# A codec kernel with a fixed task order, four groups of x per transposing transfer, a fourth residual buffer and the third tap's products on Pool

## The chip, the cores and the metric

The kernel runs on one core of one Trainium2 chip. The metric is device time in microseconds (us), from the first to the last work of one execution. Before the change three runs gave 812.22, 815.28 and 817.3 us, so the median is 815.28 us. Engines are named as in the profile: PE (TensorE matmul), PEld (its weight loads), DVE (VectorE), ACT (ScalarE), POOL (GpSimd) and SP (SyncE, which here only issues transfers).

## The reference

```python
B, T, D, K = 2, 16000, 512, 3
Nq, C = 4, 8
xp = jnp.pad(x, ((0,0),(pad,pad),(0,0)))
for i in range(K):
    z = z + xp[:, i:i+T, :] * dw_enc[i][None, None, :]
res = z = silu(z)
for s in range(Nq):
    cb = codebooks[s]
    d2 = einsum("btd,btd->bt", res, res)[..., None] - 2.0 * einsum("btd,cd->btc", res, cb) + einsum("cd,cd->c", cb, cb)
    idx = d2.argmin(-1)
    sel = cb[idx]
    q = q + sel
    res = res - sel
# qp = q padded like x
for i in range(K):
    y = y + qp[:, i:i+T, :] * dw_dec[i][None, None, :]
```

All tensors are bf16. A three-tap convolution per channel and a SiLU make z; four residual quantisers each pick the nearest of 8 code words; a second three-tap convolution per channel runs over the sum of the picked words.

## The kernel before

**Tiling.** The 32,000 tokens are cut into 250 groups of 128 tokens, token p of group g being row 250 p + g of x, so that neighbours in time lie in neighbouring groups. The groups form 17 chunks: `SIZES` gives 4, 12, fourteen times 16, and 10. Channels lie on the partitions, in four blocks of 128, so one operation on one block of a 16-group chunk has the shape 128x2048.

**Loading.** Chunks 0 and 1 come in as rows and are turned on PE. From chunk 2 on, each group is a transposing transfer of its own on SP's queue (L428), into the ring `XT` of 34 groups. When the ring wraps, POOL copies two groups to its start (L444).

**Front of a chunk**, for each of the four channel blocks: three products of x with a tap (L486: tile Z for the first, T for the second and third, all on DVE); two additions into Z or into the residual (L500 on DVE, or an accumulating transfer Z<-T that POOL issues, L497); exp on ACT (L508), plus one on DVE (L512), reciprocal on ACT (L184), and the product with that (L518 on DVE), which leaves the SiLU in a residual buffer `RES`. `SPLIT = (1, 1, 1, 2)` says how many of the two additions are transfers in each block: five of eight in a chunk, so three are L500.

**Four stages of a chunk**, one after the other, since each needs the residual of the one before. PE computes the products of each token with itself and with the code words (the scores, L590, after a mask matmul, L584), in two halves of 8 groups. ACT takes the diagonal out (L601), DVE casts the dot products (L620), PE adds up (L604, L611), DVE casts the sums (L616). POOL adds the code norms (L658), makes a small tie-break term (L645 adds a norm, L647 multiplies), and adds both (L662). DVE takes the minimum (L666) and the one-hot (L672), POOL notes it (L678). PE and ACT turn the one-hots into picks of word pairs (L715, L720, L727, L733); PE multiplies these by the code words (L749) and DVE adds the result to the residual (L755, four per stage, in stages 0 to 2). After stage 3 the one-hots are turned (L701) and PE decodes the output with two or three matmuls per group pair (L773), ACT copies it out (L779) and SP stores it (L783).

**Buffers.** `RES` is a set of three buffers. A chunk takes one at its first L500 and gives it back when its stage-3 scores are done. Z, T and E have four tiles each, PSUM four.

**Order.** `Plan` holds the tasks of all chunks with an estimated hold and delay. It steps through time and gives each free engine the ready task with the earliest due time, `START[chunk] + OFF[name]`, if its buffers are free. What comes out is a fixed order on each engine. Where PE would idle, the planner adds warm-up matmuls (L387), with `WARM = 0.4`.

Of the kernel before, what the change touches and what calls it, by code (L numbers as in the profile page):

```python
# [10 lines left out]
BF16 = mybir.dt.bfloat16  # L11
# [9 lines left out]
LC = 16  # L21
ROOM = 2 * GC + 2

SIZES = [4, 12] + [16] * 14 + [10]
# [5 lines left out]
WARM = 0.4  # L30
SPLIT = (1, 1, 1, 2)
RELU = (0, 1, 2, 3)

ZB, TB, EB, YB = 4, 4, 4, 2
# [3 lines left out]
START = [-49.78, -21.21, -11.1, 40.29, 77.41, 126.87, 171, 213.64, 259.89, 295.9, 339.35, 382.88, 414.63, 449.59, 490.48, 512.46, 542.77]  # L38
OFF = {
    "words": -209.08, "codes": -112.52, "col0": -187, "sums": -87.73, "mask": -228.88, "norms": -202.91, "col1": 18.74,  # L40
# [19 lines left out]
}  # L60


class Plan:

# [12 lines left out]
    def run(self):  # L77
# [3 lines left out]
        for n, t in enumerate(tasks):  # L81
            for d in t[3]:
                after[d].append(n)
# [789 lines left out]
```

## Time and profile before

| | |
|---|---|
| median of three runs | 815.28 us |
| the profiled execution | 809.59 us, of which its span is 807.8 us |
| busy: DVE, PE, ACT, POOL | 628.2, 622.8, 538.6, 284.9 us |
| mean granted TensorE clock | 0.897 |
| transposing transfers of x | 233, besides one for the edge |
| accumulating transfers Z<-T | 75 |
| warm-up matmuls L387 | 111 in the trace |

The busy time of an engine is the time in which at least one of its instructions runs. "us" and "xN" in a row are the busy time and the count of a group, "idle before" is the engine's idle time just ahead of it, with what ended it. In a timeline row the first number is the start, the second the length of that stretch, and a bracket holds the idle time before it. A line such as L755 is a line of the kernel before.

### The profile page before, as it was taken

The page shows a single profiled execution, that of the slowest core. Times are in us where ns is not written, and L with a number is a line of the kernel's source. Part 1 is how long each engine was busy: PE and PEld are TensorE (multiplying, and loading weights), DVE is VectorE, ACT ScalarE, POOL GpSimd, SP SyncE. Part 2 cuts the span into 40 slices and gives each one's busy share as a digit, 9 for nine tenths or more (in the row PEclk, how much of TensorE's full clock was granted, in tenths as well). Part 3 has the DMA queues.
Part 4 walks back from the last instruction along what each step waited for, and adds up shares of the span by engine and source line. Part 5 has one row for each costly group of instructions (what it writes and reads, how often), then busy time and mean ns, then how long its engine had stood idle before and what let it go on. Part 6 is the DMA issues. An engine that isn't in the chain of part 4 may idle for free.

```text
span 807.8 us, 28980 instructions
## 1 busy us (share of the span) xinstructions
PE 622.8 (77%) x13019; PEld 381.0 (47%) x13092; DVE 628.2 (78%) x1027; ACT 538.6 (67%) x571; POOL 284.9 (35%) x459
## 2 busy tenths in 40 slices
PE   3065787877878878887799877878885759889985
PEld 3023454544444544535356545554553526446543
DVE  5998889896988798878778897887969785855530
ACT  2345748494789477697847976866937596793553
POOL 1244353442534155426243452253414342212200
PEclk9568788999989999989999998998998979989989
DMA  4749677767796777895967778768984542121231
GB/s 150 112 83 153 130 133 134 124 121 164 141 207 147 164 145 175 136 176 117 166 153 121 203 139 184 128 140 153 187 158 68 105 121 93 47 92 44 80 157 79
DMA packets 149542, 107.71 MB, mean 133 GB/s; under 512 B 130217, under 2 KB 131370, under 8 KB 149290
## 3 DMA queue, kind: packets, MB, share of 16 engines
q1 hardware_dynamic: 137796, 66.62, 37.4%
q0 software_dynamic: 11472, 39.10, 27.0%
q8 instruction: 102, 1.67, 0.9%
q14 instruction: 22, 0.18, 0.1%
q10 hardware_dynamic: 150, 0.13, 0.1%
HBM read 3.70 MB, written 32.77 MB: 45 GB/s over the span
## 4 chain that ended last, share of the span: by engine, by line
PE 28%; DVE 19%; ACT 14%; issue 8%; POOL 7%; DMA 3%; ACTq 0%; another core or an unknown queue 0%; DVEq 0%; POOLq 0%
PE PS L590 12%; DVE RES L755 10%; PE PS L749 5%; ACT YSB L779 4%; PE PS L584 4%; ACT E L184 3%; PE PS L773 3%; PE PS L611 2%; ACT E L508 2%; POOL S L645 2%; ACT L L601 2%; POOL D L658 2%; DVE RES L500 2%; DMA out_dram<-YSB 2%; DVE T L486 1%
## 5 line engine op out<-in xcount | busy, mean ns | idle before, releaser
L755 DVE TENSOR_TENSOR RES<-RES,PS 128x2048 bf16<-128x2048 bf16 (+2 forms) x204 | 224.5, 1136 | 26.0 <-PE PS L749 25.6
L590 PE MATMUL PS<-RES 128*64 128x80 bf16 (+1 forms) x8064 | 204.2, 208 | 36.7 <-DVE RES L518 26.7
L590 PEld LDWEIGHTS <-RES 128*64 128x64 bf16 x8064 | 170.1, 118 | 93.9 <-issue 31.7
L601 ACT ACTIVATE L<-PS 128x512 bf16<-128x512 f32 (+2 forms) x132 | 75.8, 577 | 168.5 <-PE PS L590 90.4
L749 PE MATMUL PS<-POH,PAIR 64*128 64x512 bf16 (+2 forms) x1224 | 158.4, 396 | 33.6 <-DVE RES L755 14.6
L779 ACT ACTIVATE YSB<-PS 128x1024 bf16<-128x1024 f32 (+1 forms) x126 | 124.6, 1019 | 15.3 <-PE PS L773 8.9
L184 ACT ACTIVATE E<-E 128x2048 bf16<-128x2048 bf16 (+2 forms) x68 | 120.5, 1786 | 6.6 <-DVE E L512 6.4
L658 POOL TENSOR_TENSOR D<-VT,GPOS 128x128 bf16<-128x128 bf16 (+2 forms) x68 | 45.9, 675 | 204.1 <-DVE VT L616 204.0
L749 PEld LDWEIGHTS <-PAIR 64*128 64x128 bf16 x1224 | 61.9, 102 | 103.5 <-issue 61.4
L497 POOL DMA_DIRECT2D Z<-T x75 | 73.0, 1012 | 102.7 <-issue 28.1
L508 ACT ACTIVATE E<-RES 128x2048 bf16<-128x2048 bf16 (+2 forms) x53 | 92.3, 1755 | 15.1 <-DVE RES L500 12.7
L486 DVE TENSOR_SCALAR T<-XT,WENC 128x2048 bf16<-128x2048 bf16 (+2 forms) x136 | 98.8, 739 | 3.4 <-DMA Z<-T 3.4
L773 PE MATMUL PS<-A,OHT 128*128 128x512 bf16 x224 | 80.9, 398 | 23.6 <-ACT OHT L707 5.9
L584 PE MATMUL PS<-MASK,IDENT 128*128 128x256 bf16 (+2 forms) x264 | 76.1, 288 | 12.1 <-DVE RES L755 6.0
L678 POOL COPY OH<-OH 128x128 bf16<-128x128 bf16 (+2 forms) x68 | 37.8, 562 | 121.8 <-DVE OH L672 121.7
L620 DVE CAST PR<-PS 128x64 bf16<-128x64 f32 (+2 forms) x132 | 28.8, 220 | 65.2 <-PE PS L590 50.5
L518 DVE TENSOR_TENSOR RES<-RES,E 128x2048 bf16<-128x2048 bf16 (+2 forms) x53 | 59.0, 1123 | 8.7 <-ACT E L184 8.7
L645 POOL TENSOR_SCALAR S<-VT,GMIN 128x16 f32<-128x16 bf16 (+2 forms) x68 | 51.4, 755 | 34.6 <-DVE VT L616 34.3
L500 DVE TENSOR_TENSOR RES<-Z,T 128x2048 bf16<-128x2048 bf16 (+2 forms) x53 | 63.4, 1203 | 0.1
L773 PEld LDWEIGHTS <-OHT 128*128 128x128 bf16 x373 | 32.6, 101 | 63.4 <-issue 30.2
L486 DVE TENSOR_SCALAR Z<-XT,WENC 128x2048 bf16<-128x2048 bf16 (+2 forms) x68 | 50.1, 744 | 0.2
L611 PEld LDWEIGHTS <-L 64*64 64x64 bf16 x2016 | 38.2, 111 | 20.9 <-issue 14.3
(103 smaller groups left out, 676.3 us busy)
## 6 DMA issues: line engine op xcount, KB each, us to landing
Z<-T POOLq DMA_DIRECT2D x70, 512.0 KB, 6.0
out_dram<-YSB SPq DMA_DIRECT2D x61, 512.0 KB
XT<-in_x_dram SPq DMA_TRANSPOSE x233
Z<-T POOLq DMA_DIRECT2D x5, 384.0 KB, 5.1
RES<-in_x_dram SPq DMA_DIRECT2D x1, 1536.0 KB
YSB<-in_codebooks_dram SPq DMA_DIRECT2D x12, 64.0 KB
RES<-in_x_dram SPq DMA_DIRECT2D x1, 640.0 KB
out_dram<-YSB SPq DMA_DIRECT2D x1, 384.0 KB
```

The costliest lines, as they stand in the source:

```text
L184: nc.scalar.add_instruction(mybir.InstActivation(name=nc.get_next_instruction_name(), engine=mybir.EngineType.Activation, ins=args, outs=[ ...
L486: nc.vector.tensor_scalar(out=u[name][:, 0:G, :], in0=XT[:, i, at + k:at + k + G, :], scalar1=WENC[:, i, k:k + 1], scalar2=None, op0=ALU.mult)
L497: nc.gpsimd.dma_start(out=z, in_=t, accum_op=ALU.add)
L500: nc.vector.tensor_tensor(out=u["R"], in0=halves(u["Z"]), in1=halves(u["ZTU"[k]]), op=ALU.add)
L508: nc.scalar.activation(halves(u["E"]), halves(u["Z"]) if adds == 2 else u["R"], ACT.Exp, scale=-1.0)
L584: nc.tensor.matmul(V[:, b, :, own:own + HT], lhsT=IDENT, rhs=MASK[:, 0:m // 2, :], start=True, stop=False, skip_group_check=True)
L590: nc.tensor.matmul(V[h * HT:(h + 1) * HT, b, r, :], lhsT=half[:, LC:LC + HT], rhs=half[:, lo:hi], start=False, stop=(i == KT - 1), skip_gr ...
L601: nc.scalar.activation(u["L", q][:, 0:m, :].rearrange("p (b r) t -> p b r t", b=2), u["V", q][:, :, :, own:own + HT], ACT.Relu)
L749: nc.tensor.matmul(u["SEL", i][:, h, 0:H * HT], lhsT=PAIR[s][rows, part, i * P:(i + 1) * P], rhs=u["POH"][rows, 0:H, :], start=(part == 0) ...
L755: nc.vector.tensor_tensor(out=tokens, in0=tokens, in1=words, op=ALU.add)
L773: nc.tensor.matmul(Y[:, h, :], lhsT=lhs(), rhs=rhs, start=(a == 0), stop=(a == len(terms) - 1))
L779: nc.scalar.activation(u["YSB"][:, k:k + n, :], u[k][:, 0:n, :], ACT.Copy)
```

## The change

The planner's due times go, and the order of all tasks is written out as one list, `ORDER`. Buffers are handed out by the plan itself. Beside that:

- `JOIN = 4`: one transposing transfer brings four groups of x (59 instead of 233, besides the edge); `XT` is laid out group by group, and a transfer waits only for the readers of its own groups.
- `RESN = 4`: a fourth residual buffer. In it, the code-word columns lie between the halves of a token group and are shared by neighbours (`WD` = 80 instead of 96 columns a half); score matmuls keep their widths of 72 and 80.
- `POOLED`: in chunks 2 to 15 the products of the third tap are `nc.gpsimd.tensor_scalar`, 56 in all, 128x2048 each.
- `SPLIT`: one accumulating transfer per block instead of 1, 1, 1, 2; the second addition is always on DVE.
- E has no tiles of its own: exp writes to Z. Z has seven tiles, T four.
- The code norms stand in the tile PR, so that the tie-break needs one POOL operation instead of two.
- `CASTS`: in stages 0 and 2 ACT casts the dot products, in 1 and 3 DVE; one cast covers ten columns instead of eight.
- `WARM = 0`: no warm-up matmuls. Exps of a chunk wait for all reciprocals of the chunk before, so ACT loads 33 tables instead of 47.
- Setup: code columns are written by ACT, PSUM is zeroed once by DVE, some setup operations are joined.

```diff
-WARM = 0.4
-SPLIT = (1, 1, 1, 2)
-ZB, TB, EB, YB = 4, 4, 4, 2
+WARM = 0.0
+SPLIT = ((0, 0, 0, 0), (0, 0, 0, 0), (1, 1, 1, 1), (1, 1, 1, 1))
+POOLED = ((0, 0, 0, 0), (0, 0, 0, 0), (1, 1, 1, 1), (0, 0, 0, 0))
+JOIN = 4
+CASTS = (True,False,True,False)
+PSB, ZB, TB, YB, LB, POHB, RESN = 4, 7, 4, 2, 2, 2, 4
-START = [-49.78, -21.21, -11.1, 40.29, 77.41, 126.87, 171, 213.64, 259.89, 295.9, 339.35, 382.88, 414.63, 449.59, 490.48, 512.46, 542.77]
+ORDER = """
+0 40 26 36 28 38 14 8 349 351 353 15 9 350 352 179 355 354 356 1 43 41 42 45 16 17 46 3 44 10 11 4 47 37 48 70 71 49 27 63 50 51 52 64 65 66 56 186
...
+        order = [int(n) for n in ORDER.split()]
+        for n in order:
+            engine, hold, delay, needs, _, emit, take, give, use = self.tasks[n]
+            begin = max([until.get(engine, 0.0)] + [end[d] for d in needs])
+            for k in take:
+                at, self.held[n, k] = free[k].pop(min(range(len(free[k])), key=lambda j: free[k][j][0]))
+                begin = max(begin, at)
...
-        def one(n):
-            nc.sync.dma_start_transpose(out=XT[:, :, at + n, :], in_=group_rows(g0 + n - 1))
+        def some(n, m):
+            nc.sync.dma_start_transpose(out=XT[:, at + n:at + n + m, :, :].rearrange("p n k t -> p (n k) t"),
+                                        in_=bass.AP(tensor=xf.tensor, offset=xf.offset + (g0 + n - 1) * D, ap=[[S * D, P], [1, m * D]]))
...
             def product(k):
-                nc.vector.tensor_scalar(out=u[name][:, 0:G, :], in0=XT[:, i, at + k:at + k + G, :], scalar1=WENC[:, i, k:k + 1],
-                                        scalar2=None, op0=ALU.mult)
+                (nc.gpsimd if k == 2 and pooled else nc.vector).tensor_scalar(out=plan.held[u[k], "Z" if k == 0 else "T"][:, 0:G, :], in0=XT[:, at + k:at + k + G, i, :],
+                                        scalar1=WENC[:, i, k:k + 1], scalar2=None, op0=ALU.mult)
...
         def dots(q, m):
-            nc.vector.tensor_copy(u["PR"][:, q:q + m, 0:C].rearrange("p (b r) c -> p b r c", b=2), u["V", q][:, :, :, pick:pick + C])
+            src = banked(q, m // 2 + 1)[:, :, :, at:at + C]
+            dst = held(first, f"PR{s}")[:, q // m, :, 0:m // 2 + 1, 0:C]
+            if CASTS[s]:
+                nc.scalar.activation(dst, src, ACT.Copy)
+            else:
+                nc.vector.tensor_copy(dst, src)
...
         def ties():
-            u["S"] = small.tile([P, GC], F32, name="S")
-            nc.gpsimd.tensor_scalar(out=u["S"][:, 0:G], in0=u["TR"][:, 0:G], scalar1=GMIN[:, s:s + 1], scalar2=None, op0=ALU.add)
-            u["T"] = small.tile([P, GC, C], F32, name="T")
-            nc.gpsimd.tensor_tensor(out=u["T"][:, 0:G, :], in0=u["S"][:, 0:G].to_broadcast([P, G, C]),
-                                    in1=STEP.rearrange("p (o c) -> p o c", o=1).to_broadcast([P, G, C]), op=ALU.mult)
+            u["KEY"] = small.tile([P, GC, C], F32, name="KEY")
+            nc.gpsimd.tensor_tensor(out=u["KEY"][:, 0:G, :], in0=u["VT"][:, 0:G, C:].to_broadcast([P, G, C]),
+                                    in1=STEP.rearrange("p (o c) -> p o c", o=1).to_broadcast([P, G, C]), op=ALU.mult)
```

**DVE in the middle of the program, before.** A row is a line, an operation, and out<-in with the shape; T_6812 and the like are single tiles.

```order
L672 TENSOR_TENSOR OH_6804<-T,M 128x2x8x8
L486 TENSOR_SCALAR T_6812<-XT,WENC 128x2048
L486 TENSOR_SCALAR Z<-XT,WENC 128x2048
L486 TENSOR_SCALAR T_6857<-XT,WENC 128x2048
L666 TENSOR_REDUCE M<-T 128x16
L616 CAST VT<-PS 128x144
L672 TENSOR_TENSOR OH_6873<-T,M 128x2x8x8
L512 TENSOR_SCALAR E<-E 128x2048
L486 TENSOR_SCALAR T_6886<-XT,WENC 128x2048
L486 TENSOR_SCALAR T_6896<-XT,WENC 128x2048
L518 TENSOR_TENSOR RES_105<-RES_105,E 128x32x64
```

**The same engine, now**, with L544 for L486, L558 for L500, L575 for L518 and L813 for L755:

```order
L813 TENSOR_TENSOR RES_138<-RES_138,PS_90 128x32x64
L575 TENSOR_TENSOR RES_137<-RES_137,Z_104 128x32x64
L544 TENSOR_SCALAR Z_104<-XT,WENC 128x2048
L718 TENSOR_REDUCE M<-KEY 128x16
L721 TENSOR_TENSOR OH_131<-KEY,M 128x2x8x8
L575 TENSOR_TENSOR RES_137<-RES_137,Z_109 128x32x64
L674 CAST PR_125<-PS_91 128x10x8
L544 TENSOR_SCALAR Z_109<-XT,WENC 128x2048
L558 TENSOR_TENSOR RES_138<-Z_106,T_113 128x32x64
L544 TENSOR_SCALAR T_113<-XT,WENC 128x2048
L813 TENSOR_TENSOR RES_139<-RES_139,PS_91 128x32x64
```

Two products per block stand here instead of three, and the residual buffers are now four (RES_137 to RES_140) where there were three (RES_103 to RES_105).

**POOL in the middle of the program, before:**

```order
L497 DMA Z<-T_6812 128x2048
L658 TENSOR_TENSOR D_6876<-VT,GPOS 128x128
L678 COPY OH_124<-OH_6873 128x16x8
L645 TENSOR_SCALAR S<-VT,GMIN 128x16
L647 TENSOR_TENSOR T<-S,STEP 128x128
L497 DMA Z<-T_6886 128x2048
L662 TENSOR_TENSOR T<-D_6876,T 128x128
```

**POOL now**, with L556 for L497, L706 for L658, L710 for L647, L714 for L662 and L728 for L678:

```order
L544 TENSOR_SCALAR T_112<-XT,WENC 128x2048
L556 DMA Z_103<-T_110 128x2048
L710 TENSOR_TENSOR KEY<-VT,STEP 128x128
L706 TENSOR_TENSOR D_6120<-VT,GPOS 128x128
L544 TENSOR_SCALAR T_110<-XT,WENC 128x2048
L714 TENSOR_TENSOR KEY<-D_6120,KEY 128x128
L728 COPY OH_126<-OH_131 128x16x8
```

The 128x2048 products stand between the small operations of the stages, here even between two of one stage, and L645 is gone.

More of the change, by code (lines that the diff above doesn't have):

```diff
@@ L415, in load_rows @@
-        st["loaded"] = moved + (chunks[0]["loaded"] if st["n"] else [])
-        if st["n"]:
-            codes.append(plan.add("DVE", 1.2, 1.4, moved + codes[0:1], (1, "col2"), lambda: code_columns(RESB[2])))
+            t = took[i] = plan.add("PE", 0.12 * N, 0.12 * N + 0.2, [rows], (n, "rows"), lambda i=i: turn(i), take=("ps",))
+            dve = i % 2 and n == 0
+            hold = (0.08 if dve else 0.12) * N
+            moved.append(plan.add("DVE" if dve else "ACT", hold, hold + 0.1, [t], (n, "rows"), lambda i=i: move(i), give=((t, "ps"),)))
@@ L419, in load @@
+        st["loaded"] = moved + (chunks[0]["loaded"] if n else [])
+        if n:
+            codes[2] = plan.add("ACT", 2.0, 2.2, moved + [words], (1, "col2"), lambda: code_columns(RESB[2]))
+    reads = {p: [] for p in range(ROOM)}
     def load(st):
@@ L552, in block @@
-            return rest
+                    t = plan.add("POOL", 0.9, 0.9, needs, due, lambda: total(k))
+                    return plan.add("DMA", 3.0 * f, 3.0 * f + 2.0, [t], due, None, give=give)
+                first = k == 2 and "RES" not in st
+                if k == 2:
+                    needs = needs + [st["RES"] if not first else chunks[n - 1]["RES"] if 0 < n < RESN else None]
+                t = plan.add("DVE", dve(1.13), dve(1.13) + 0.1, needs, due,
+                             lambda: total(k), take=("RES",) if first else (), give=give)
@@ new lines, in add_up @@
+                if first:
+                    st["RES"] = t
+                return t
+            hold, delay = dve(0.66), dve(0.66) + 0.1
+            for k in range(2):
+                u[k] = plan.add("DVE", hold, delay, st["loaded"], (n, f"{'ztu'[k]}{i}"), lambda k=k: product(k), take=("ZT"[k],))
+            a = add_up(1, [u[0], u[1]])
+            u[2] = plan.add("POOL" if pooled else "DVE", 0.1 + 2.2 * f if pooled else hold, 0.2 + 2.2 * f if pooled else delay, st["loaded"] + [u[1]], (n, f"u{i}"),
+                            lambda: product(2), take=("T",))
```

662 lines of the change are left out of this document (309 added, 353 removed), and 112 rows, old and new, of tables (OFF, ORDER).

## The prediction

> **What bounds the kernel now.** I read the busy times first. No engine is full over the whole span, so I cut the span at the last product of a tap, which is where DVE's front work ends (a chunk's E, reciprocals and SiLUs follow, but no new chunk).
>
> ```profile
> PE 622.8 (77%) x13019; PEld 381.0 (47%) x13092; DVE 628.2 (78%) x1027; ACT 538.6 (67%) x571; POOL 284.9 (35%) x459
> ...
> 678.63 0.61 DVE L486 TENSOR_SCALAR T<-XT,WENC 128x1536 bf16<-128x1536 bf16 x1
> ...
> 0.00:54.00 54.00, 17.79 (x144) 11.29 (x145) 44.59 (x120) 14.68 (x17) 14.30 (x33) 0.72 0.54 118
> 54.00:679.00 625.00, 494.11 (x10668) 303.73 (x10725) 522.44 (x798) 450.29 (x458) 248.02 (x364) 0.90 0.75 145
> 679.00:808.00 129.00, 110.94 (x2216) 65.95 (x2222) 61.22 (x111) 73.68 (x98) 22.55 (x63) 0.94 0.22 83
> ```
>
> The last three rows give, for each stretch, the busy time of PE, PEld, DVE, ACT and POOL, then the clock, the share of the DMA engines and GB/s. Up to 679 us DVE is the fullest engine: 44.6 + 522.4 = 567.0 us, which leaves it idle for 112 us or 16.5%. PE has 511.9 us there. After 679 us PE is at 86% and DVE at 47%, so the tail of 129 us is PE's.
>
> Why is DVE idle at all while there is always another chunk to start? Three times I looked at where a chunk gives back its residual buffer, by its last stage-3 scores on PE (L590), and where the third chunk after it takes it, by its first addition on DVE (L500).
>
> ```profile
> 284.53 0.77 PE L590 MATMUL PS<-RES 128*64 128x80 bf16 x32
> 285.47 1.34 DVE L500 TENSOR_TENSOR RES<-Z,T 128x2048 bf16<-128x2048 bf16 x1
> ...
> 426.01 0.77 PE L590 MATMUL PS<-RES 128*64 128x80 bf16 x32
> 426.95 1.22 DVE L500 TENSOR_TENSOR RES<-Z,T 128x2048 bf16<-128x2048 bf16 x1
> ...
> 552.24 0.94 PE L590 MATMUL PS<-RES 128*64 128x80 bf16 x32
> 553.37 2.35 DVE L500 TENSOR_TENSOR RES<-Z,T 128x2048 bf16<-128x2048 bf16 x2
> ```
>
> The scores end at 285.30, 426.78 and 553.18, and the additions start 0.17 to 0.19 us later. Buffers go from hand to hand with nothing between: **three residual buffers gate the chunks**. DVE can be fuller than it is on average:
>
> ```profile
> 120.00:140.00 20.00, 16.14 (x320) 10.35 (x322) 19.09 (x29) 17.92 (x19) 7.75 (x10) 0.85 0.67 122
> 200.00:220.00 20.00, 16.55 (x318) 9.24 (x318) 19.37 (x31) 13.34 (x15) 11.52 (x16) 0.97 0.66 130
> ```
>
> In these stretches it is busy for 19.09 and 19.37 of 20 us, so idle for 3 to 5%.
>
> **The change part by part.** I sum DVE's work up to the last product, turn it into time by the share that DVE idles, and add PE's tail.
>
> ```profile
> L486 DVE TENSOR_SCALAR T<-XT,WENC 128x2048 bf16<-128x2048 bf16 x112 | 85.7, 777 | 3.4 <-DMA Z<-T 3.4
> L500 DVE TENSOR_TENSOR RES<-Z,T 128x2048 bf16<-128x2048 bf16 x42 | 54.5, 1304 | 0.1
> L620 DVE CAST PR<-PS 128x64 bf16<-128x64 f32 x112 | 24.8, 223 | 53.4 <-PE PS L590 42.8 <-ACT L L601 10.1
> L250 DVE COPY RES<-CBT 128x2048 bf16<-128x2048 bf16 x3 | 3.1, 1039 | 0.0
> L249 DVE COPY RES<-CBT 128x2048 bf16<-128x2048 bf16 x3 | 2.3, 778 | 0.0
> ```
>
> - Third tap to POOL: 56 products x 0.777 = 43.5 us less.
> - One more addition on DVE in each of chunks 2 to 15 (four instead of three): 14 x 1.304 = 18.3, and about 1 in the last, smaller chunk: 19.3 us more.
> - Casts of two of four stages to ACT: 56 x 0.223 for the full chunks and some 1.6 for the small ones: 14.1 us less.
> - Code columns to ACT: 5.4 us less; zeroing PSUM has no row, and I take back 3.4 us for it. Together 2 us less. The other setup edits I set at nothing.
>
> That makes 567.0 - 43.5 + 19.3 - 14.1 - 2.0 = 526.7 us.
>
> Now the price of a product on POOL. The nearest operation is POOL's copy within XT, with one input and bf16 on both sides; further off are two-input operations.
>
> ```profile
> L444 POOL COPY XT<-XT x7: 1027/1037/2072, 54.4 to 551.5; 128x1024 bf16<-128x1024 bf16 x7
> ...
> 421.94 0.29 POOL L678 COPY OH<-OH 128x128 bf16<-128x128 bf16 x1 [4.42 <-DVE OH L672]
> ...
> 286.94 0.42 POOL L662 TENSOR_TENSOR T<-D,T 128x128 f32<-128x128 bf16 x1
> ...
> 72.32 1.15 POOL L343 TENSOR_TENSOR PAIR<-YSB,PAIR 128x512 bf16<-128x512 f32 x1 [4.47 <-DVE YSB L342]
> ```
>
> From 128 to 1024 columns a copy goes from 0.29 to 1.03 us, 0.82 ns a column, so 2048 columns are about 1.9 us. Two-input operations go from 0.42 at 128 to 1.15 at 512, 1.9 ns a column, so about 4.1 us at 2048. I take 2.0 us, near the copy, and keep both ends.
>
> Such a product also holds DVE up. Three long POOL operations of before, each with the DVE instruction that ran into it:
>
> ```profile
> 287.31 1.03 POOL L444 COPY XT<-XT 128x1024 bf16<-128x1024 bf16 x1
> 287.60 1.83 DVE L500 TENSOR_TENSOR RES<-Z,T 128x2048 bf16<-128x2048 bf16 x1
> ...
> 466.77 1.03 POOL L444 COPY XT<-XT 128x1024 bf16<-128x1024 bf16 x1
> 467.05 1.29 DVE L512 TENSOR_SCALAR E<-E 128x2048 bf16<-128x2048 bf16 x1
> ...
> 73.44 1.71 POOL L344 TENSOR_TENSOR PAIR<-YSB 128x512 bf16<-128x512 f32 x1
> 73.94 2.28 DVE L500 TENSOR_TENSOR RES<-Z,T 128x2048 bf16<-128x2048 bf16 x1
> ...
> 431.91 0.68 DVE L512 TENSOR_SCALAR E<-E 128x2048 bf16<-128x2048 bf16 x1
> ```
>
> Alone an L500 takes 1.22 us (the row at 426.95) and an L512 0.68. So DVE lost 0.61, 0.61 and 1.06 us: each time it ended its own length after POOL had ended, as if it had not started before. Updates that read PSUM (L755) show nothing of the kind:
>
> ```profile
> L755 DVE TENSOR_TENSOR RES<-RES,PS 128x2048 bf16<-128x2048 bf16 x168 | 198.1, 1214 | 17.6 <-PE PS L749 17.1
> ```
>
> The Trainium skill ("SBUF — State Buffer", section "SBUF: two separate sides") has a rule that fits and speaks against this change: DVE operations in a two-port mode or with two SBUF inputs and GpSimd operations take one port pair as an exclusive lock, whole instructions at a time. The rows above agree (0.61, 0.61 and 1.06 us). Its "GPSIMD Engine Reference", section 3.1, gives about 1.03 cycles an element at 1.2 GHz for a light one-input loop, from which 2048 elements are an estimated 1.8 us; by that the sum would be an estimated 56 x 0.2 / 0.91 = 12 us lower.
>
> The instruction that meets POOL had lost 0.4 to 0.65 us less than POOL's length. For 2.0 us that is a stall of 1.4 us when a product is met. Of DVE's time up to the last product about a third is updates and casts, which don't mind, so some products pass unseen. I take **1.2 us per product**, 56 x 1.2 = 67 us; bounds are 0 (all under updates and idle time) and the full 2.0 (112 us; with 4.1 us a product, 230 us). DVE then has 526.7 + 67 = 594 us, 27 more than before.
>
> Against that stands the fourth buffer. With gaps of 0.2 us at the handing over, a fourth one lets a chunk start its additions when it is ready. I let DVE's idle share fall from 16.5% to 9%, between that and the 3 to 5% of the full stretches: 594 / 0.91 = 653 us to the last product, instead of 679.
>
> **The tail.** In the new order 36 updates stand behind the last product on DVE, as before, and as many decode matmuls are left, so PE's tail stays. The warm-up matmuls go:
>
> ```profile
> L387 PE MATMUL PS<-CB,IDENT 128*128 128x512 bf16 x17 | 5.1, 393 | 1.1 <-ACT YSB L779 1.0
> ```
>
> That is the row for 679 to 808 us: 5.1 us, mostly in gaps; I take 4 us off, 125 us.
>
> Span: 653 + 125 = 778 us. The profiled execution took 809.59 us for a span of 807.8, so 780 us; the median of the runs is 815.28 / 809.59 = 1.007 of it, which gives **785 us**.
>
> **Costed at nothing, with their cover.** PE needs 512 us up to the last product, about 35 less without warm-ups; in 653 us it would be 73% busy. ACT gets 64 casts and the code columns and loses 14 table loads. Both have room: 450 us busy in the 625 us of the middle stretch. If ACT's casts come late, PE's L604 waits.
>
> POOL loses L645 and 15 transfers and gets 56 x 2.0 = 112 us, so it goes from 285 to some 330 to 400 us with its own waits. But its products stand among the operations of the stages:
>
> ```profile
> L645 POOL TENSOR_SCALAR S<-VT,GMIN 128x16 f32<-128x16 bf16 x56 | 44.7, 799 | 26.7 <-DVE VT L616 26.4
> ```
>
> Each stage saves up to 0.8 us and waits now and then up to 2 us behind a product; with four chunks under way I set these against each other.
>
> Transposing transfers:
>
> ```profile
> L428 SPq DMA_TRANSPOSE XT<-in_x_dram x233: 1190/1269/3372, 23.0 to 604.2; - x117
> ```
>
> SP spent 1.27 us on each of 233. With four groups the issue lies between 1.3 us (4 per chunk) and four times that (the same in all); both are off the path, since the row of L486 above names a wait for Z<-T and none for a transfer of x. A transfer of four must wait for the readers of four groups; what is late then is the next chunk's first product, and with a chunk and a half of Z tiles under way I see no wait.
>
> **The rivals.**
>
> - *The port lock takes the gain back* (slower). Every product on POOL meets DVE and costs its full 2.0 us: 526.7 + 112 = 639 us. At the idle share of before, 16.5%, that is 765 + 125 = 890; at 9%, 702 + 125 = 827 us, 835 as a median. The same happens at 1.2 us if the idle share does not fall: 594 / 0.835 = 711 + 125 = 836, 844 as a median. For it speaks that two of my three rows lost all but 0.4 us; against it that L755 has the most DVE time and loses nothing. It decides from an idle share of 13% (at 1.2 us) upward.
> - *The stalls fall under updates and idle time* (much faster). At 0.5 us per product DVE has 555 us; at 9% idle 610 + 125 = 735, 742 as a median. For it speaks that idle time on DVE, 112 us, can take stalls for nothing.
> - *Both cancel* (no change): DVE idles 13%, 594 / 0.87 = 683 + 125 = 808 us. That is also what comes out if the fourth buffer does not do what it should because the order, or the seven Z tiles that now hold E too, gate the chunks in its place.
>
> **How the numbers follow.** Forecast 785 us, chance 0.42 (765 to 805). Much faster 0.16, cancelled 0.14, slower 0.28. The range must reach to both outer cases: from 738 to 848 us. A difference of 1% is about what a measurement of this kernel can tell from none; by the cases faster has 0.58, the same 0.14, slower 0.28.
>
> **What would show it.** L544 on POOL at 1.9 to 2.3 us at its shortest; L558, L569 and L575 on DVE with a mean 0.2 to 0.4 us above their shortest, L813 unchanged; DVE busy some 590 us up to its last product, near 653 us; additions into a residual buffer that start well after its last scores. I am wrong if POOL's products take 4 us, if DVE waits for them through the Z-tile sum instead, or if the buffers still go from hand to hand.

## The result, and the profile after

The changed kernel took **912.07 us** (median of four runs, 909.83 to 914.93), against 815.89 us for the kernel before in the runs beside it. The ratio is 1.118, with a 95% interval from 1.113 to 1.123. The forecast was 785 us, with a range from 738 to 848. The profiled execution took 910.08 us, its span is 908.2.

First the page and the stretches of the changed kernel, cut again at the last product of a tap (791 us). The columns of the stretches are those of the prediction.

```profile
PE 621.7 (68%) x13031; PEld 383.2 (42%) x13031; DVE 766.4 (84%) x891; ACT 545.6 (60%) x640; POOL 547.6 (60%) x439
```

```profile
0.00:791.00 791.00, 517.67 (x10768) 320.89 (x10770) 708.47 (x792) 475.51 (x536) 528.07 (x389) 0.85 0.53 113
791.00:908.00 117.00, 104.02 (x2275) 62.34 (x2268) 57.94 (x100) 70.11 (x105) 19.52 (x50) 0.98 0.23 88
```

Up to the last product DVE is busy for 708.5 us, where it was 567.0 before and 526.7 by the forecast. It is idle for 82.5 us or 10.4%; before it was 112 us. So the 112 us that this part grew (679 to 791) are 141 more of busy DVE and 29 less of idle DVE. The tail shrank from 129 to 117 us.

What POOL's and DVE's products took stands in the view of their source line (shortest, median, longest in ns):

```profile
L544 DVE TENSOR_SCALAR T<-XT,WENC x80: 344/744/6686, 20.8 to 790.6; 128x2048 bf16<-128x2048 bf16 x56, 128x1536 bf16<-128x1536 bf16 x16, 128x512 bf16<-128x512 bf16 x8
L544 DVE TENSOR_SCALAR Z<-XT,WENC x68: 349/746/5919, 20.5 to 772.7; 128x2048 bf16<-128x2048 bf16 x56, 128x1536 bf16<-128x1536 bf16 x8, 128x512 bf16<-128x512 bf16 x4
L544 POOL TENSOR_SCALAR T<-XT,WENC x56: 5427/5730/7447, 53.3 to 746.3; 128x2048 bf16<-128x2048 bf16 x56
```

POOL's products take **5.43 us at their shortest**, not 1.9 to 2.3. And DVE's own products, 0.74 us as a median, take up to 6.7 us. The groups of DVE, shapes kept apart, tell which operations grew:

```profile
L813 DVE TENSOR_TENSOR RES<-RES,PS 128x2048 bf16<-128x2048 bf16 x168 | 199.7, 1213 | 23.0 <-PE PS L807 17.9 <-ACT Y L841 3.7 <-ACT OHT L781 1.0
L575 DVE TENSOR_TENSOR RES<-RES,Z 128x2048 bf16<-128x2048 bf16 x56 | 100.1, 1794 | 6.0 <-ACT RES L303 3.5 <-ACT Z L220 2.6
L558 DVE TENSOR_TENSOR RES<-Z,T 128x2048 bf16<-128x2048 bf16 x56 | 96.5, 1731 | 13.6 <-POOL T L544 12.0 <-PE PS L661 1.6
L544 DVE TENSOR_SCALAR T<-XT,WENC 128x2048 bf16<-128x2048 bf16 x56 | 81.6, 1462 | 0.0
L544 DVE TENSOR_SCALAR Z<-XT,WENC 128x2048 bf16<-128x2048 bf16 x56 | 67.4, 1212 | 0.1
```

L813, the update that reads PSUM, takes 1213 ns, as it did before (1214). The four groups below it read and write SBUF alone, and their means are far above what such operations took before (777 ns for a product, 1304 for an addition, in the prediction's rows). Note where the stall is *not* visible: the wait for POOL's result (L558, 12.0 us in all) is small. The stall sits inside the busy time of DVE's instructions, so no list of waits shows it. One such meeting, from the timeline:

```profile
448.77 6.52 POOL L544 TENSOR_SCALAR T<-XT,WENC 128x2048 bf16<-128x2048 bf16 x1
...
449.99 0.27 DVE L718 TENSOR_REDUCE M<-KEY 128x16 f32<-128x128 f32 x1
...
450.18 5.66 DVE L544 TENSOR_SCALAR T<-XT,WENC 128x2048 bf16<-128x2048 bf16 x1
```

POOL's product ends at 455.29. DVE's product, 0.75 us alone, starts at 450.18 and ends at 455.84. For 4.9 us the kernel's fullest engine stood still. Not every operation within SBUF is stopped: the minimum (L718) got through in its usual 0.27 us while the product ran, and the longest of its 68 instructions took 0.29 us.

### The profile page after: what moved, and what is told of

The parts are those of the page before. It is cut to its first block, busy times and chain, and to the rows that moved or that the text cites. A ratio compares the mean times of both kernels' runs of the same rounds, so it can differ in the third digit from the quotient of the medians.

```text
span 908.2 us, 28840 instructions
## 1 busy us (share of the span) xinstructions
PE 621.7 (68%) x13031; PEld 383.2 (42%) x13031; DVE 766.4 (84%) x891; ACT 545.6 (60%) x640; POOL 547.6 (60%) x439
## 4 chain that ended last, share of the span: by engine, by line
DVE 41%; PE 23%; POOL 18%; issue 7%; ACT 7%; DMA 3%; ACTq 0%; DVEq 0%; SPq 0%; POOLq 0%
POOL T L544 12%; DVE RES L813 9%; DVE T L544 7%; PE PS L807 6%; PE PS L661 6%; PE PS L837 5%; DVE Z L544 5%; DVE RES L558 5%; DVE RES L575 4%; DVE Z L569 4%; DVE OH L721 3%; POOL KEY L710 2%; ACT Y L841 2%; PE PS L655 2%; POOL D L706 2%
## 5 line engine op out<-in xcount | busy, mean ns | idle before, releaser
L544 POOL TENSOR_SCALAR T<-XT,WENC 128x2048 bf16<-128x2048 bf16 x56 | 325.1, 5854 | 1.0 <-DMA Z<-T 1.0
L813 DVE TENSOR_TENSOR RES<-RES,PS 128x2048 bf16<-128x2048 bf16 (+2 forms) x204 | 226.0, 1134 | 33.2 <-PE PS L807 28.0
L841 ACT ACTIVATE Y<-PS 128x1024 bf16<-128x1024 f32 (+1 forms) x126 | 125.2, 1018 | 65.5 <-PE PS L837 54.4
L566 ACT ACTIVATE Z<-RES 128x2048 bf16<-128x2048 bf16 (+2 forms) x68 | 120.5, 1784 | 33.8 <-DVE RES L558 33.6
L220 ACT ACTIVATE Z<-Z 128x2048 bf16<-128x2048 bf16 (+2 forms) x68 | 120.2, 1784 | 29.3 <-DVE Z L569 29.1
L575 DVE TENSOR_TENSOR RES<-RES,Z 128x2048 bf16<-128x2048 bf16 (+2 forms) x68 | 113.4, 1675 | 6.0 <-ACT RES L303 3.5
L556 POOL DMA_DIRECT2D Z<-T x60 | 56.5, 965 | 101.6 <-ACT Y L841 17.7
L558 DVE TENSOR_TENSOR RES<-Z,T 128x2048 bf16<-128x2048 bf16 (+2 forms) x68 | 105.5, 1563 | 13.7 <-POOL T L544 12.0
L837 PE MATMUL PS<-A,FIN 128*128 128x512 bf16 x249 | 91.6, 415 | 17.8 <-DVE RES L813 12.5
L706 POOL TENSOR_TENSOR D<-VT,GPOS 128x128 bf16<-128x128 bf16 (+2 forms) x68 | 40.0, 589 | 100.3 <-DVE VT L701 100.3
L544 DVE TENSOR_SCALAR T<-XT,WENC 128x2048 bf16<-128x2048 bf16 (+2 forms) x80 | 100.1, 1260 | 0.0
L710 POOL TENSOR_TENSOR KEY<-VT,STEP 128x128 f32<-128x128 bf16 (+2 forms) x68 | 44.2, 651 | 74.5 <-DVE VT L701 74.4
L544 DVE TENSOR_SCALAR Z<-XT,WENC 128x2048 bf16<-128x2048 bf16 (+2 forms) x68 | 74.0, 1095 | 0.1
L569 DVE TENSOR_SCALAR Z<-Z 128x2048 bf16<-128x2048 bf16 (+2 forms) x68 | 67.2, 995 | 2.4 <-ACT Z L566 2.4
L728 POOL COPY OH<-OH 128x128 bf16<-128x128 bf16 (+2 forms) x68 | 39.3, 580 | 43.0 <-DVE OH L721 41.5
```

Of the source, the lines that this page charges most:

```text
L220: nc.scalar.add_instruction(mybir.InstActivation(name=nc.get_next_instruction_name(), engine=mybir.EngineType.Activation, ins=args, outs=[ ...
L544: (nc.gpsimd if k == 2 and pooled else nc.vector).tensor_scalar(out=plan.held[u[k], "Z" if k == 0 else "T"][:, 0:G, :], in0=XT[:, at + k:a ...
L558: nc.vector.tensor_tensor(out=residual(), in0=halves(z()), in1=halves(t), op=ALU.add)
L566: nc.scalar.activation(halves(e()), halves(z()) if adds == 2 else residual(), ACT.Exp, scale=-1.0)
L569: nc.vector.tensor_scalar(out=e()[:, 0:G, :], in0=e()[:, 0:G, :], scalar1=1.0, scalar2=None, op0=ALU.add)
L575: nc.vector.tensor_tensor(out=residual(), in0=halves(z()) if adds == 2 else residual(), in1=halves(e()), op=ALU.mult)
```

## The experiments

**1. What do the 56 products on POOL cost?** The changed kernel with only the third tap put back on DVE:

```diff
-POOLED = ((0, 0, 0, 0), (0, 0, 0, 0), (1, 1, 1, 1), (0, 0, 0, 0))
+POOLED = ((0, 0, 0, 0), (0, 0, 0, 0), (0, 0, 0, 0), (0, 0, 0, 0))
```

> The changed kernel with all third-tap products back on DVE, in the same places of the task order; everything else stays. Theory (the products on POOL cost the time, by their length of 5.43 us and by what DVE waits for them): DVE works 527 + 44 = 571 us up to its last product, at 10% idle that is 634 us, with a tail of 118 us 752 us, so 740 to 785 us or 0.91 to 0.96 of the kernel before. Rival (the new order, the buffers or the transfers of four cost the time): above 880 us still.

It took 762.81 us (761.65 to 765.38), 0.933 of the kernel before (0.928 to 0.938). That is faster than both kernels: the rest of the change brings 7%, the products on POOL cost 149 us. Its stretches and four of its groups:

```profile
0.00:643.00 643.00, 487.89 (x10730) 309.45 (x10783) 567.99 (x849) 474.40 (x536) 214.50 (x333) 0.85 0.65 139
643.00:760.00 117.00, 101.89 (x2244) 62.05 (x2251) 57.62 (x99) 69.85 (x105) 19.56 (x50) 0.98 0.23 88
```

```profile
L544 DVE TENSOR_SCALAR T<-XT,WENC 128x2048 bf16<-128x2048 bf16 x112 | 83.6, 765 | 0.0
L558 DVE TENSOR_TENSOR RES<-Z,T 128x2048 bf16<-128x2048 bf16 x56 | 69.2, 1243 | 0.3
L575 DVE TENSOR_TENSOR RES<-RES,Z 128x2048 bf16<-128x2048 bf16 x56 | 68.3, 1225 | 4.0 <-ACT RES L303 2.6 <-ACT Z L220 1.3
L544 DVE TENSOR_SCALAR Z<-XT,WENC 128x2048 bf16<-128x2048 bf16 x56 | 42.6, 769 | 0.1
```

DVE without the third tap's 56 products is 568.0 - 56 x 0.765 = 525.2 us up to the last product; the prediction's sum, without its stall, was 526.7. With the products on POOL it was 708.5, so each product cost DVE (708.5 - 525.2) / 56 = 3.27 us where doing it itself costs 0.765. Most of this stands in the four groups: with the third tap's products taken out of the row of T (83.6 / 2 = 41.8 us), they grew by 31.8, 27.3, 39.8 and 24.8 us, together 123.7 of the 183.3 us.

**2. Does the cost go with the number of products?** Two of the four blocks on POOL:

```diff
-POOLED = ((0, 0, 0, 0), (0, 0, 0, 0), (1, 1, 1, 1), (0, 0, 0, 0))
+POOLED = ((0, 0, 0, 0), (0, 0, 0, 0), (1, 0, 1, 0), (0, 0, 0, 0))
```

> The changed kernel with the third-tap products of two of the four channel blocks on POOL (28 instead of 56). Theory (a price per product): halfway between the changed kernel and the one with none on POOL, 820 to 845 us, with DVE's loss again near 3.25 us per product. Rival (POOL's queue as a whole is the bound, so that the loss sets in only above a certain load): less than a third of the loss comes back with half of the products, so below 800 us.

844.45 us. The stretch up to the last product:

```profile
0.00:725.00 725.00, 512.82 (x10706) 322.94 (x10761) 642.34 (x820) 474.55 (x536) 375.32 (x361) 0.79 0.57 124
```

That is (642.3 - 568.0 + 28 x 0.765) / 28 = 3.42 us of DVE for each of the 28. With 56 it was 3.27, so the cost is one of each product, not of a crowded POOL.

**3. The joined transfers.** Four transfers of one group instead of one of four, products left on POOL:

```diff
-            nc.sync.dma_start_transpose(out=XT[:, at + n:at + n + m, :, :].rearrange("p n k t -> p (n k) t"),
-                                        in_=bass.AP(tensor=xf.tensor, offset=xf.offset + (g0 + n - 1) * D, ap=[[S * D, P], [1, m * D]]))
+            for j in range(m):
+                nc.sync.dma_start_transpose(out=XT[:, at + n + j, :, :], in_=group_rows(g0 + n + j - 1))
```

> The changed kernel with each transposing transfer of four groups issued as four of one group, at the same place. Theory (the transfers do not matter): 905 to 920 us, the same within 1%. Rival (transfers of four come late or block stores behind them): below 890 us.

927.9 us, 1.7% more, where 905 to 920 had been expected and the rival asked for less than 890. The joined transfers did no harm; in this single run they rather helped.

**4. The disputed price by itself.** Ahead of all tasks, operations one after the other on POOL, then on DVE alone, then the same beside a product on POOL; the rest is the changed kernel.

```diff
+        for _ in range(2):
+            nc.gpsimd.tensor_scalar(out=TT[0], in0=XT[:, 0:GC, 0, :], scalar1=w, scalar2=None, op0=ALU.mult)
+        for _ in range(2):
+            nc.gpsimd.tensor_scalar(out=TT[0], in0=Z[0], scalar1=w, scalar2=None, op0=ALU.mult)
...
+        for _ in range(2):
+            nc.gpsimd.tensor_copy(TT[0], Z[0])
+        for _ in range(2):
+            nc.gpsimd.tensor_tensor(out=TT[0], in0=Z[0], in1=Z[1], op=ALU.mult)
```

> The changed kernel with a probe ahead of its tasks: POOL operations of 128x2048 alone, then four DVE operations each alone and each just after a POOL product has started. Theory (the product's own program is slow, and DVE operations with two SBUF inputs or a doubled read port wait for its end): 5.4 us for the product alone from either layout, 2.7 us at half the size, the copy near 1.9 us; DVE's product and its sum of two SBUF tiles take some 5 us beside it, the sum with a PSUM input and the cast from PSUM their own length. Rival (the layout of XT or DVE's traffic makes it slow): about 2 us from a contiguous tile, or about 2 us with DVE idle.

The timeline of the added operations ("x2": two of them and a gap of some 0.1 us between):

```profile
13.79 10.97 POOL L924 TENSOR_SCALAR T<-XT,WENC 128x2048 bf16<-128x2048 bf16 x2 [5.66 <-DVE WENC L255]
24.86 10.97 POOL L926 TENSOR_SCALAR T<-Z,WENC 128x2048 bf16<-128x2048 bf16 x2
35.92 5.78 POOL L928 TENSOR_SCALAR T<-Z,WENC 128x1024 bf16<-128x1024 bf16 x2
41.76 3.84 POOL L930 COPY T<-Z 128x2048 bf16<-128x2048 bf16 x2
45.69 8.17 POOL L932 TENSOR_TENSOR T<-Z,Z 128x2048 bf16<-128x2048 bf16 x2
...
54.23 0.75 DVE L936 TENSOR_SCALAR Z<-Z,WENC 128x2048 bf16<-128x2048 bf16 x1
55.01 1.23 DVE L938 TENSOR_TENSOR Z<-Z,Z 128x2048 bf16<-128x2048 bf16 x1
56.27 0.55 DVE L940 TENSOR_TENSOR Z<-Z,PS 128x768 bf16<-128x768 bf16 x1
...
58.80 0.17 DVE L951 COPY OH<-Z 128x16 bf16<-128x16 bf16 x1 [1.76 <-ACT Z L944]
...
59.28 5.45 POOL L953 TENSOR_SCALAR T<-XT,WENC 128x2048 bf16<-128x2048 bf16 x1
...
59.63 5.64 DVE L936 TENSOR_SCALAR Z<-Z,WENC 128x2048 bf16<-128x2048 bf16 x1
...
65.77 5.46 POOL L953 TENSOR_SCALAR T<-XT,WENC 128x2048 bf16<-128x2048 bf16 x1
...
66.14 4.45 DVE L938 TENSOR_TENSOR Z<-Z,Z 128x2048 bf16<-128x2048 bf16 x1
...
71.55 5.46 POOL L953 TENSOR_SCALAR T<-XT,WENC 128x2048 bf16<-128x2048 bf16 x1
...
71.92 0.54 DVE L940 TENSOR_TENSOR Z<-Z,PS 128x768 bf16<-128x768 bf16 x1
72.49 4.54 DVE L951 COPY OH<-Z 128x16 bf16<-128x16 bf16 x1
```

With nothing beside it, one product on POOL takes 5.44 us, in the layout of XT as well as contiguous, and 2.84 us at half the width: 2.53 ns for each further column. The copy takes 1.89 us and the two-input product 4.05 us, so both ends that the prediction set (1.9 and 4.1) were right for the operations they came from, and the operation itself lies outside them. Beside a product on POOL, DVE's product goes from 0.75 to 5.64 us, its sum of two SBUF tiles from 1.23 to 4.45, and a copy of 16 columns from 0.17 to 4.54. The sum with a PSUM input does not change (0.55, 0.54).

**5. Was only the price wrong?** The same kernel with an operation of the length that the prediction had assumed: POOL copies the columns and leaves the multiplication by the weight out.

```diff
-                (nc.gpsimd if k == 2 and pooled else nc.vector).tensor_scalar(out=plan.held[u[k], "Z" if k == 0 else "T"][:, 0:G, :], in0=XT[:, at + k:at + k + G, i, :],
+                if k == 2 and pooled:
+                    nc.gpsimd.tensor_copy(plan.held[u[k], "T"][:, 0:G, :], XT[:, at + k:at + k + G, i, :])
+                    return
+                nc.vector.tensor_scalar(out=plan.held[u[k], "Z" if k == 0 else "T"][:, 0:G, :], in0=XT[:, at + k:at + k + G, i, :],
```

> The changed kernel in which GpSimd only copies the third tap's columns of x into T (128x2048, the same shape, places and waits) and leaves out the multiplication by the tap's weight in chunks 2 to 15: 1.89 us alone instead of 5.44. It is the length of operation that the prediction was made for. Theory (the length of the GpSimd operation sets the loss of VectorE, 3.25 us per product of 5.44 us, so 1.13 us per copy): VectorE busy to the last product 526.7 + 56 x 1.13 = 590 us, at 10 to 12% idle 655 to 670, and 117 behind it: a span of 772 to 787, time 775 to 790, as predicted for the change itself. Rival (each operation of GpSimd costs VectorE a fixed wait, whatever its length): about 910. Second rival (the order of the tasks was changed, and that costs): well over 790 with VectorE's mean durations as in the kernel with the third tap back on VectorE.

787.94 us, where the prediction had said 785 for the change itself. Both rivals fell. Its stretches, and the source line of the copies:

```profile
0.00:668.00 668.00, 494.32 (x10707) 313.19 (x10762) 587.37 (x792) 474.07 (x536) 319.62 (x389) 0.83 0.64 134
668.00:785.00 117.00, 102.31 (x2265) 62.48 (x2276) 58.04 (x100) 70.23 (x105) 19.49 (x50) 0.99 0.23 88
```

```profile
L545 POOL COPY T<-XT x56: 1879/2159/2975, 53.0 to 625.0; 128x2048 bf16<-128x2048 bf16 x56
```

The loss is (587.4 - 525.2) / 56 = 1.11 us per copy, with 1.2 in the prediction.

**6. A length in between.** The products on POOL as a two-input operation, x times the weight spread over the columns:

```diff
+                    nc.gpsimd.tensor_tensor(out=plan.held[u[k], "T"][:, 0:G, :], in0=XT[:, at + k:at + k + G, i, :],
+                                            in1=WENC[:, i, k:k + 1].rearrange("p (g o) -> p g o", g=1).to_broadcast([P, G, P]), op=ALU.mult)
```

> The changed kernel with the products on GpSimd written as an operation of two inputs, x times the tap's weight spread over the columns: 4.05 us alone if the spread weight costs what a second tile costs, against 5.44 for the product by a scalar. Theory (the length sets VectorE's loss, 0.6 us per us of GpSimd as in the runs at 1.89 and 5.44): 2.4 us per product, 526.7 + 135 = 662 us busy, at 10.4% idle 738, and 117 behind it: span 855, time 858. Rival (the scalar, which GpSimd reads per partition, is not what makes the product long, and the spread weight costs the same): 5.4 us in the rows and a time of 900 to 925.

858.75 us, where 858 had been expected. The same product, written in another way, is 53 us cheaper:

```profile
L545 POOL TENSOR_TENSOR T<-XT,WENC 128x2048 bf16<-128x2048 bf16 x56 | 214.7, 3889 | 15.3 <-DVE RES L562 8.4 <-DMA Z<-T 6.9
```

```profile
0.00:740.00 740.00, 515.90 (x10784) 322.74 (x10784) 662.16 (x794) 476.40 (x536) 419.06 (x389) 0.81 0.56 121
```

(662.2 - 525.2) / 56 = 2.45 us per product.

**7. Next to nothing on POOL.** One of the 16 token groups is multiplied, the others left out; T is zeroed once, which costs DVE 3.6 us.

```diff
+                g1 = 1 if k == 2 and pooled else G
```

> The changed kernel with GpSimd multiplying one of the 16 token groups of each third-tap product (128x128 in place of 128x2048), the other 15 left out in chunks 2 to 15 (T is set to zero once ahead of the tasks): what an almost free offload would be worth. Theory (VectorE bounds the part up to the last product): 526.7 us and 56 stalls of 0.3 us = 543 us busy, at 10.4 to 11.7% idle 607 to 615, and 117 behind it: a span of 724 to 732. Rival (with the products gone another engine binds, ScalarE with its 545 us above all): VectorE's idle share rises over 15% and the span stays at 750 or more.

745.66 us, between the theory (a span of 724 to 732) and its rival (750), at a span of 743.7:

```profile
0.00:627.00 627.00, 483.99 (x10731) 307.45 (x10784) 540.84 (x798) 472.99 (x536) 261.42 (x389) 0.90 0.69 143
```

DVE's busy time came as expected (541, with 543 expected), its idle share did not fall further but rose to 13.7%. So even this nearly free offload is worth only about 17 us against experiment 1: DVE's work fell by 27 us, and 11 of them came back as idle time (75 to 86 us).

Experiments 5 to 7 and the change make one table, with the 525.2 us of experiment 1 as its zero (loss per operation as above, in experiment 7 without the 3.6 us of zeroing):

```profile
L545 POOL TENSOR_SCALAR T<-XT,WENC 128x128 bf16<-128x128 bf16 x56 | 59.2, 1072 | 27.1 <-DMA Z<-T 22.9 <-DVE RES L559 4.2
```

```profile
L544 POOL TENSOR_SCALAR T<-XT,WENC 128x2048 bf16<-128x2048 bf16 x56 | 325.1, 5854 | 1.0 <-DMA Z<-T 1.0
```

These rows are the first and the last line of the table, of experiment 7 and of the changed kernel.

| on POOL, 56 times | mean length there, us | DVE busy to the last product | loss per operation, us | loss / length | DVE idle |
|---|---|---|---|---|---|
| one group of the product | 1.07 | 540.8 | 0.21 | 0.20 | 13.7% |
| copy | 2.15 | 587.4 | 1.11 | 0.52 | 12.1% |
| two-input product | 3.89 | 662.2 | 2.45 | 0.63 | 10.5% |
| product by a scalar (the change) | 5.85 | 708.5 | 3.27 | 0.56 | 10.4% |

In the three rows from 2.15 us on, DVE loses a little over half of what POOL's operation lasts. Handing over pays only where the loss is less than the 0.765 us which the product costs on DVE. On a straight line between the first two rows that is an estimated 1.7 us on POOL; a line between the times of the two runs (745.66 and 787.94 us) meets the 762.81 us of experiment 1 at an estimated 1.5.

**8. Where else could the product go?** The third tap on DVE but for one of four blocks, which ScalarE multiplies:

```diff
+                if k == 2 and pooled:
+                    nc.scalar.activation(plan.held[u[k], "T"][:, 0:G, :], XT[:, at + k:at + k + G, i, :], ACT.Copy, scale=WENC[:, i, k:k + 1])
+                    return
```

> The third tap back on VectorE, but the product of one of the four blocks of chunks 2 to 15 on ScalarE (14 products, an activation with the tap's weight as its scale, about 1.9 us each from the copy measured there): VectorE loses 14 x 0.745 = 10.4 us, ScalarE gains 26.7 us on 544. Theory (VectorE bounds, ScalarE has room and no shared port): 10.4/0.883 = 11.8 us off 762.8, so 751 us, ratio 0.92. Rival (ScalarE's exps and copies for the output come late behind the products): 763 or more, ratio 0.935 to 0.96.

773.27 us (0.945 of the kernel before, 0.937 to 0.953), 10 us more than with all of the third tap on DVE. DVE was relieved, but its idle share went up from 11.7 to 14.3%, in part by waits for that very product. The stretch up to the last product, and the addition into the residual buffer (L561 in this kernel):

```profile
0.00:653.00 653.00, 487.10 (x10700) 310.79 (x10754) 559.63 (x834) 498.42 (x550) 213.94 (x333) 0.86 0.63 137
```

```profile
L561 DVE TENSOR_TENSOR RES<-Z,T 128x2048 bf16<-128x2048 bf16 (+2 forms) x68 | 78.8, 1169 | 8.4 <-ACT T L545 8.1
```

**9. What lowered DVE's idle share?** The prediction had put it down to the fourth residual buffer. First, three buffers in place of four in the kernel of experiment 1; a task that finds none is put behind the others.

```diff
-    plan.free["RES"] = list(RESB)
+    plan.free["RES"] = RESB[0:3]
...
-        for n in order:
+        left, done = list(order), set()
+        while left:
+            n = next(n for n in left if all(d in done for d in self.tasks[n][3]) and all(free[k] for k in self.tasks[n][6]))
+            left.remove(n)
+            done.add(n)
```

> The kernel with the third tap back on VectorE (762.8 us) with three residual buffers in place of four; a task that needs one is put behind the others until one is free. Theory (three buffers gate the chunks, as read from the kernel before, where VectorE stood idle 16.5% of the time): 571 us busy at 16.5% idle is 684 us, and 118 behind it: a span of 802. Rival (the fourth buffer is worth nothing, the gain is the casts on ScalarE and the transfers): 755 to 770.

987.5 us: far beyond both. DVE is busy as before and idle for a third of the time:

```profile
0.00:854.00 854.00, 501.94 (x10670) 319.67 (x10724) 570.00 (x845) 474.69 (x533) 187.45 (x333) 0.77 0.48 105
```

The written-out order needs four buffers, but this says little of what the buffer is worth, since a list made for four is a bad list for three. Then the casts: on DVE in all stages, and on ScalarE in all.

```diff
-CASTS = (True,False,True,False)
+CASTS = (False,False,False,False)
```

> The kernel with the third tap back on VectorE (762.8 us) with the casts of the dot products of all four stages on VectorE. Theory (VectorE's work up to the last product decides): 15.7 us more of casts (66 of 0.238), over 0.883 some 17 us more: 780. Rival (the casts sit in VectorE's idle time, and ScalarE is relieved): 755 to 766.

> The kernel with the third tap back on VectorE, with the casts of the dot products of all four stages on ScalarE. Theory (VectorE decides): 15.7 us of casts go, over 0.883 some 17 us less: 746. Rival (ScalarE, in whose one queue the casts stand behind exps of 1.78 us, passes the wait on to the next matmuls): 763 to 775.

All on DVE: 819.86 us, 1.007 of the kernel before (1.003 to 1.011), so 57 us more than with two stages on ScalarE, where 17 had been expected. All on ScalarE: 772.41 us (0.945, 0.939 to 0.951), 10 us more, where 17 less had been expected; that is the rival's 763 to 775. The first, with four residual buffers, joined transfers and no product on POOL, has the idle share of the kernel before (16.2%, with 16.5):

```profile
0.00:690.00 690.00, 506.43 (x10717) 314.86 (x10718) 578.35 (x905) 467.48 (x479) 212.11 (x334) 0.83 0.61 130
690.00:815.00 125.00, 108.58 (x2315) 64.56 (x2313) 59.17 (x108) 70.22 (x96) 18.92 (x50) 0.96 0.21 82
```

DVE's work grew by only 10 us up to the last product, its idle time by 37, and the tail by 8 (125 us). Much of the idle time stands ahead of the casts. Over the whole span, the prediction's row of L620 has 53.4 us there for the kernel before; in experiment 1 and in this run it is

```profile
L674 DVE CAST PR<-PS 128x80 bf16<-128x80 f32 x56 | 13.0, 239 | 24.1 <-ACT L L665 17.0 <-PE PS L661 6.9
```

```profile
L674 DVE CAST PR<-PS 128x80 bf16<-128x80 f32 x112 | 26.2, 242 | 48.2 <-ACT L L665 25.1 <-PE PS L661 22.8
```

Ahead of the additions into the residual buffers there is next to none in any of the three: 0.1 (L500, in the prediction), 0.3 (L558 in experiment 1) and 1.1 us (here). In the list of waits (us in total, times, longest), ScalarE's copies of the diagonal stand behind DVE's casts, so the two engines also hold each other up:

```profile
ACT L L665 <- DVE PR L674: 93.7, 40, 7.2
```

In the kernel of experiment 1 the same row is less than a third:

```profile
ACT L L665 <- DVE PR L674: 28.5, 16, 6.6
```

Last, a like move in the kernel before, with its planner and three buffers (casts of stages 1 and 2 on ScalarE, not 0 and 2):

```diff
+            if s in (1, 2):
+                nc.scalar.activation(dst, src, ACT.Copy)
+            else:
+                nc.vector.tensor_copy(dst, src)
```

> The kernel before (single transfers, three residual buffers, planner) with the casts of the dot products of two of the four stages (1 and 2) on ScalarE; the planner orders the tasks anew by the same due times. Theory (the casts are what frees the stages, since with all casts on VectorE the changed kernel without products on GpSimd has the idle share of the kernel before): the same 40 to 55 us as there, 760 to 775. Rival (three residual buffers hold the chunks, so the casts give back only VectorE's own 14.1 us, over 0.835): 798. Second rival (the order around the casts decides, and due times written for other casts fit them badly): 816 or more.

846.11 us, 1.038 of the kernel before (1.029 to 1.047). The theory fell, and so did its first rival; the second, that the order around the casts decides, had asked for 816 or more. Up to the last product, now at 713 us, DVE's busy time fell by 5 us and its idle share rose to 21%:

```profile
0.00:713.00 713.00, 523.47 (x11017) 319.08 (x11082) 562.45 (x868) 486.40 (x546) 263.97 (x402) 0.87 0.70 136
```

The casts that stayed on DVE have 53.8 us of idle time ahead of them there, as all of them had before (53.4). Where the casts stand is worth tens of us, but by these runs only together with the order around them. How much of the lower idle share belongs to the fourth buffer and how much to the written-out order isn't settled: a fourth buffer in the kernel before was not tried.

## Why the prediction was wrong

**The step that failed is the price of a product on POOL.** "From 128 to 1024 columns a copy goes from 0.29 to 1.03 us ... I take 2.0 us, near the copy, and keep both ends." The operation measured 5.44 us by itself and 5.85 in the kernel, above the upper end of 4.1. The prediction had named products of 4 us as a sign of being wrong. The error was one of kind: from the number of inputs the prediction took a product by a scalar to lie between a copy and a two-input operation. It lies above both (1.89, 4.05, 5.44).

The Trainium skill's "GPSIMD Engine Reference", section 3.1, from which the prediction had an estimate of 1.8 us for a light one-input loop, fits the copy (1.89 us) and not the product by a scalar; the measurement decides.

**The stall followed the prediction's rule, at that price.** It had set 1.2 us for an operation of 2.0, or 0.6 of the length. Measured was 0.56 for the product, 0.63 for the two-input one and 0.52 for the copy. With 5.85 us the prediction's own sum would have been 526.7 + 56 x 3.5 = 723 us, at 9% idle 795, and 125 behind it: a span of 920, against 908.2. (Updates and casts, which are not stopped, are 223 of DVE's 567 us up to the last product before, so 39% and not "about a third"; the rule was coarse.) Experiment 5 shows it from the other side: with an operation of 2 us the kernel takes 788 us. The faster rival, stalls that fall under updates and idle time, needed a loss of 0.5 us for 2.0; it fell in the runs with 2 us and more on POOL (1.11 to 3.27 us lost).

**The slower rival was right in kind and too small.** "The port lock takes the gain back" came to 835 and 844 us because it too was worked out at 2.0 us a product. Its one larger sum, a span of 890 at the idle share of before, stands in the prediction, and yet the range ended at 848. The 4.1 us end, which the prediction had priced at 230 us of stall, was left out of range and rival alike; with it the case "slower" would have had, at 9% idle, a span of (526.7 + 230) / 0.91 + 125 = 957 us. Both ends of a bound have to be carried to the end.

On the mechanism: the Trainium skill's "SBUF — State Buffer", section "SBUF: two separate sides", speaks of an exclusive lock held for whole instructions. DVE's product and small copies agree (0.75 to 5.64 us, 0.17 to 4.54), and operations with a PSUM input pass, as the prediction had read from L755. The sum of two SBUF tiles agrees in part: it ended at 70.59 us, 0.64 ahead of POOL's product at 71.23. This is no accident of one row: in the changed kernel 22 of the 24 sums (L558, L575) that a product stopped ended 0.64 or 0.65 us ahead of it (one at 431.31 + 3.47 = 434.78 us, the product at 429.99 + 5.44 = 435.43), while in the prediction's row at 287.31 the sum ended 1.09 us after POOL's copy, and beside the two-input product of experiment 6 most ended 1.08 or 1.09 after it. So beside a product by a scalar a two-input operation is let go some 1.7 us before the product's recorded end; why was not tried.

**DVE's other terms were right as a sum.** It was 526.7 us, and 525.2 came out: products, the fourth addition, the casts and the setup together.

**The idle share came out near the forecast, but the reason given for it is not shown.** Forecast were 9%, and 10.4% came out. The prediction had given this to the fourth residual buffer, and experiment 9 shows that this buffer is not enough: 16.2% with four buffers, when the casts stand on DVE. What the buffer is worth by itself stays open. Besides, a share was the wrong measure: in the changed kernel and in experiments 1, 2 and 5 to 7 DVE was idle for 75 to 86 us up to the last product, whatever POOL did, and the share is lower where that stretch is longer. So part of the nearness is luck.

One reading of the prediction was wrong here: buffers that go from hand to hand don't show that they gate. Its own row of L500 has 0.1 us of idle time ahead of all 42 additions, and its row of L620 has 53.4 us ahead of the casts, of which it used only the length. In the changed kernel an addition can still be found right at the hand-over:

```profile
437.39 1.27 PE L661 MATMUL PS<-RES 128*64 128x80 bf16 x32
438.93 1.24 PE L661 MATMUL PS<-RES 128*64 128x80 bf16 x32
440.05 1.23 DVE L558 TENSOR_TENSOR RES<-Z,T 128x2048 bf16<-128x2048 bf16 x1 [1.04 <-PE PS L661]
```

This addition starts as a chunk's last scores end, and yet all waits of L558 for scores come to 1.6 us (its row in the section on the result).

**The tail** was 117 us with 125 forecast. In experiments 1, 2 and 5 to 8 it was about 117 us too, with and without products on POOL, so those have no part in it. With all casts on DVE (experiment 9) it was 125.

**What was costed at nothing:** the joined transfers held (experiment 3). What POOL's stage operations lose behind a product wasn't told apart from DVE's own loss. The casts on ScalarE were credited with DVE's 14.1 us alone, and were worth 57 in this order. That is too little for the casts; if the buffer was credited with as much too much, two errors hid each other, but what the buffer is worth was not measured.

## What to carry to other kernels

Before an operation goes from VectorE to GpSimd, find that very operation in a trace, with its kind of operands, or measure it: on GpSimd a product by a scalar cost 2.9 times a copy of the same shape. Then count what the offload costs the engine it was to relieve; here that was 0.52 to 0.63 of GpSimd's time for operations of 2 us and more, it stood in no list of waits but in the growth of mean over usual durations, and the offload would have paid only below an estimated 1.5 to 1.7 us on GpSimd for an operation of 0.77 us on VectorE. And carry both ends of an unknown price through to the range, also the one that looks unlikely.

## What the runs showed of the hardware that was not expected

- GpSimd's product of bf16 by a scalar held per partition takes 5.44 us for 128x2048 (2.53 ns for each further column), longer than a product of two whole tiles (4.05 us). Written with the weight spread over the columns it took 3.89 us in the kernel.
- While it runs, VectorE is stopped even for a copy of 16 columns (4.54 us instead of 0.17), but not for a minimum over 128 f32 columns (0.27 us, at most 0.29). Its sums of two SBUF tiles get out 0.64 us ahead of the product's end, where beside a copy on GpSimd they end 1.09 us after it; why was not tried.
- Moving the casts of two of four stages from VectorE to ScalarE was worth 57 us in one order of tasks (stages 0 and 2) and cost 29 in another (stages 1 and 2).
